# Polysketch attention with a gated causal convolution: contiguous loads, block transposes, 8-wide denominators, convolution on TensorE, and one written order of all steps

## The chip, the cores and the metric

The kernel runs on one core of a Trainium2 chip. The metric is the device time of one launch in microseconds (us). A core has five engines with their own instruction streams: TensorE (PE in the profile, with weight loads as PEld), VectorE (DVE), ScalarE (ACT), GpSimd (POOL) and SyncE (SP), which here issues the transfers. The profile counts sixteen DMA engines, which move the data. A transfer is started by an issue, an instruction on the queue of one engine; the data move afterwards. "SPq" and the like in a chain of waits is the time in which an engine's sequencer issues or holds instructions, as opposed to the data moving ("DMA"). PSUM holds the tiles into which the kernels have TensorE write; the changed kernel calls them banks. The profile also gives the clock that TensorE's throttle granted, 1.00 being full speed. The texts call 1.00 an open gate and 0.50 half clock.

Runs are labelled fast or slow, slow here being over 1.5% above the fastest of the same kernel.

## The reference, cut to what matters

```python
# q, k, v: (batch 4, heads 4, tokens 1088, dim 32); S1, S2: (8, 32)
def phi(x):                                   # 8 x 8 = 64 features a token and head
    a = einsum('rd,bhsd->bhsr', S1, x)
    b = einsum('rd,bhsd->bhsr', S2, x)
    return einsum('bhsi,bhsj->bhsij', a, b).reshape(..., 64)

q_p, k_p = phi(q), phi(k)
kv  = einsum('bhsf,bhsd->bhfd', k_p, v)       # 64 x 32 a head
z   = sum(k_p, axis=2)                        # 64 a head
num = einsum('bhsf,bhfd->bhsd', q_p, kv)
den = einsum('bhsf,bhf->bhs', q_p, z)[..., None] + 1e-06
x   = (num / den) -> (batch, tokens, 4 heads * 32 = 128)

gate = sigmoid(causal depthwise convolution of x, 5 taps per channel)
out  = (gate * (x @ w_val)) @ w_out           # float32, (4, 1088, 128)
```

The denominator has more structure than it shows: sum over i and j of a_i b_j z_ij is sum over i of a_i c_i with c = z b. So 64 products and a sum a token and head become 8, if c comes from a small product. The change uses this.

## The kernel before

Each batch is cut into nine chunks of up to 128 tokens. A chunk is loaded with tokens on partitions, in runs of 32 floats (128 bytes), transposed on TensorE and projected on TensorE. VectorE forms the 64 features per head, and TensorE sums k features times v over the chunks:

```python
for i in range(n_chunks):                      # 9 chunks a batch
    ...
    nc.sync.dma_start(out=q_shd[:sl, :, :], in_=src_q)      # 128-byte runs; k, v alike
    ...
    nc.tensor.transpose(k_dhs_p, k_shd..., identity32)      # float32 on TensorE
    nc.scalar.copy(out=k_dhs, in_=k_dhs_p)
    nc.tensor.matmul(ab_k_p[:sl, :], lhsT=k_dhs[:, :sl], rhs=S_blk)
    ...
    nc.vector.tensor_mul(k_p[:sl], a_bc[:sl], b_bc[:sl])
    for g in range(2):
        nc.tensor.matmul(kv_psums[g], lhsT=k_p..., rhs=v_ahd..., start=(i == 0), ...)
```

Only then, with z spread to all partitions, come the denominators, one reduction of 64 elements for each chunk and head, and the scaled features:

```python
for i in range(n_chunks):
    for h in range(H):
        nc.vector.tensor_tensor_reduce(out=tmp[:sl], in0=q_p_chunk[:sl, h, :],
                                       in1=z_bc[:sl, h, :], ..., accum_out=den[:sl, h : h + 1])
    nc.vector.reciprocal(rden[:sl], den[:sl])
    for h in range(H):
        nc.vector.tensor_scalar_mul(qps[:sl, h], q_p_chunk[:sl, h, :], rden[:sl, h : h + 1])
    for g in range(2):
        nc.tensor.transpose(qpt_p, qps..., identity)
        nc.scalar.copy(out=qpt_store[:, g, s0 : s0 + P], in_=qpt_p)
```

The convolution, the gate and the output of all four batches come at the end, the convolution as five passes over 1088 tokens on VectorE.

Of the kernel before, what the change touches and what calls it, by code (L numbers as in the profile page):

```python
# [13 lines left out]
ACT = mybir.ActivationFunctionType  # L15


@with_exitstack
def kernel(
# [12 lines left out]
    nc = tc.nc  # L32

# [4 lines left out]
    R2 = r * r  # L38
    HD = H * D
    Dm = moe_w_val.shape[0]  # L40
    assert Dm == HD == 128
    Kconv = moe_conv_w.shape[0]

    P = 128
    n_chunks = (S + P - 1) // P
    Sp = n_chunks * P
    chunk_sizes = [min(P, S - i * P) for i in range(n_chunks)]

    const = ctx.enter_context(tc.tile_pool(name="const", bufs=1))
    tmp_pool = ctx.enter_context(tc.tile_pool(name="tmp", bufs=2))  # L50
    sb = ctx.enter_context(tc.tile_pool(name="sb", bufs=5))
    psum = ctx.enter_context(tc.tile_pool(name="psum", bufs=5, space=bass.MemoryType.PSUM))
    kv_psum_pool = ctx.enter_context(tc.tile_pool(name="kv_psum", bufs=1, space=bass.MemoryType.PSUM))
    out_psum_pool = ctx.enter_context(
        tc.tile_pool(name="out_psum", bufs=1, space=bass.MemoryType.PSUM)
    )
    xpool = ctx.enter_context(tc.tile_pool(name="xpool", bufs=3))
    xsb_pool = ctx.enter_context(tc.tile_pool(name="xsb", bufs=B))

    def ptile(shape, dt=F32, tag="p0"):  # L60
        return psum.tile(shape, dt, tag="p0", name="p0")

    identity = const.tile([P, P], BF16)
    make_identity(nc, identity)
    identity32 = const.tile([P, P], F32)
    make_identity(nc, identity32)

    s1_sb = tmp_pool.tile([P, D], F32)
    nc.any.memset(s1_sb, 0.0)
    nc.sync.dma_start(out=s1_sb[:r, :], in_=S1)  # L70
    s1T_p = ptile([D, r], F32)
    nc.tensor.transpose(s1T_p, s1_sb[:r, :D], identity32[:r, :r])

    s2_sb = tmp_pool.tile([P, D], F32)
    nc.any.memset(s2_sb, 0.0)
    nc.sync.dma_start(out=s2_sb[:r, :], in_=S2)
    s2T_p = ptile([D, r], F32)
    nc.tensor.transpose(s2T_p, s2_sb[:r, :D], identity32[:r, :r])

    s12T = const.tile([D, 2 * r], F32)  # L80
    nc.vector.tensor_copy(out=s12T[:, :r], in_=s1T_p)
    nc.vector.tensor_copy(out=s12T[:, r:], in_=s2T_p)

    S_blk = const.tile([P, H * 2 * r], F32)
    nc.any.memset(S_blk, 0.0)
    for h in range(H):
        nc.sync.dma_start(
            out=S_blk[h * D : (h + 1) * D, h * 2 * r : (h + 1) * 2 * r],
            in_=s12T[:, :],
        )  # L90

    ones_row = const.tile([1, P], F32)
    nc.any.memset(ones_row, 1.0)

    w_val_sb = const.tile([Dm, Dm], BF16)
    nc.gpsimd.dma_start(out=w_val_sb, in_=moe_w_val)
    w_out_sb = const.tile([Dm, Dm], BF16)
    nc.gpsimd.dma_start(out=w_out_sb, in_=moe_w_out)

    conv_w_in = tmp_pool.tile([P, Dm], F32)  # L100
    nc.any.memset(conv_w_in, 0.0)
    nc.sync.dma_start(out=conv_w_in[:Kconv, :], in_=moe_conv_w)
    conv_wT_p = ptile([Dm, Kconv], F32)
    nc.tensor.transpose(
        conv_wT_p, conv_w_in[:Kconv, :Dm], identity32[:Kconv, :Kconv]
    )
    conv_wT = const.tile([Dm, Kconv], F32)
    nc.vector.tensor_copy(out=conv_wT, in_=conv_wT_p)

    eps = 1e-6  # L110

    x_sbs = []

    for b in range(B):
        kv_psums = [
            kv_psum_pool.tile([P, 2 * (D + 1)], F32, tag=f"kvp{g}", name=f"kvp{g}")
            for g in range(2)
        ]
        q_p_store = sb.tile([P, n_chunks, H, R2], F32, tag="qp_store")
        qpt_store = xpool.tile([P, 2, Sp], BF16, tag="qpt_store")  # L120

        for i in range(n_chunks):
            s0 = i * P
            sl = chunk_sizes[i]

            q_shd = sb.tile([P, H, D], F32, tag="q_shd")
            k_shd = sb.tile([P, H, D], F32, tag="k_shd")
            v_ahd = sb.tile([P, H, D + 1], F32, tag="v_ahd")
            if sl < P:
                nc.any.memset(q_shd, 0.0)  # L130
                nc.any.memset(k_shd, 0.0)
            nc.any.memset(v_ahd, 0.0)  # L132
            nc.gpsimd.memset(v_ahd[:sl, :, D : D + 1], 1.0)  # L133

            src_q = q[b, :, s0 : s0 + sl, :].transpose([1, 0, 2])
            src_k = k[b, :, s0 : s0 + sl, :].transpose([1, 0, 2])
            src_v = v[b, :, s0 : s0 + sl, :].transpose([1, 0, 2])
            nc.sync.dma_start(out=q_shd[:sl, :, :], in_=src_q)
            nc.sync.dma_start(out=k_shd[:sl, :, :], in_=src_k)
            nc.sync.dma_start(out=v_ahd[:sl, :, :D], in_=src_v)  # L140

            q_dhs_p = ptile([P, P], F32, tag="tp")
            nc.tensor.transpose(q_dhs_p, q_shd.rearrange("s h d -> s (h d)"), identity32)  # L143
            q_dhs = sb.tile([P, P], F32, tag="q_dhs")
            nc.scalar.copy(out=q_dhs, in_=q_dhs_p)  # L145

            k_dhs_p = ptile([P, P], F32, tag="tp")
            nc.tensor.transpose(k_dhs_p, k_shd.rearrange("s h d -> s (h d)"), identity32)  # L148
            k_dhs = sb.tile([P, P], F32, tag="k_dhs")
            nc.scalar.copy(out=k_dhs, in_=k_dhs_p)  # L150

            ab_q_p = ptile([P, H * 2 * r], tag="ab")
            nc.tensor.matmul(ab_q_p[:sl, :], lhsT=q_dhs[:, :sl], rhs=S_blk)  # L153
            ab_k_p = ptile([P, H * 2 * r], tag="ab")
            nc.tensor.matmul(ab_k_p[:sl, :], lhsT=k_dhs[:, :sl], rhs=S_blk)  # L155

            ab_q_ap = ab_q_p.rearrange("s (h rr) -> s h rr", h=H)
            b_q = sb.tile([P, H, r], F32, tag="b_q")
            nc.scalar.copy(out=b_q[:sl], in_=ab_q_ap[:sl, :, r:])  # L159
            q_p = q_p_store[:, i, :, :].rearrange("s h (i j) -> s h i j", i=r)  # L160
            a_bc = ab_q_ap[:, :, :r].unsqueeze(3).to_broadcast([P, H, r, r])
            b_bc = b_q[:, :, :].unsqueeze(2).to_broadcast([P, H, r, r])
            nc.vector.tensor_mul(q_p[:sl], a_bc[:sl], b_bc[:sl])  # L163

            ab_k_ap = ab_k_p.rearrange("s (h rr) -> s h rr", h=H)
            b_k = sb.tile([P, H, r], F32, tag="b_k")
            nc.scalar.copy(out=b_k[:sl], in_=ab_k_ap[:sl, :, r:])  # L167
            k_p = sb.tile([P, H, r, r], F32, tag="k_p")
            a_bc = ab_k_ap[:, :, :r].unsqueeze(3).to_broadcast([P, H, r, r])
            b_bc = b_k[:, :, :].unsqueeze(2).to_broadcast([P, H, r, r])  # L170
            nc.vector.tensor_mul(k_p[:sl], a_bc[:sl], b_bc[:sl])  # L171

            for g in range(2):
                nc.tensor.matmul(  # L174
                    kv_psums[g],
                    lhsT=k_p[:sl, 2 * g : 2 * g + 2, :, :].rearrange(
                        "s h i j -> s (h i j)"
                    ),
                    rhs=v_ahd[:sl, 2 * g : 2 * g + 2, :].rearrange("s h d -> s (h d)"),
                    start=(i == 0),  # L180
                    stop=(i == n_chunks - 1),
                    skip_group_check=True,
                )

        kv_bbs = [sb.tile([P, D], BF16, tag=f"kvbb{g}", name=f"kvbb{g}") for g in range(2)]
        z_col = sb.tile([P, 2], F32, tag="z_col")
        for g in range(2):
            nc.scalar.copy(out=kv_bbs[g][:R2, :], in_=kv_psums[g][:R2, :D])
            nc.scalar.copy(out=kv_bbs[g][R2:, :], in_=kv_psums[g][R2:, D + 1 : 2 * D + 1])
            nc.vector.tensor_copy(out=z_col[:R2, g : g + 1], in_=kv_psums[g][:R2, D : D + 1])  # L190
            nc.vector.tensor_copy(out=z_col[R2:, g : g + 1], in_=kv_psums[g][R2:, 2 * D + 1 : 2 * D + 2])

        z_p = ptile([2, P], F32, tag="tp")
        nc.tensor.transpose(z_p, z_col, identity32)
        z_p_sb = sb.tile([2, P], F32, tag="z_p_sb")
        nc.vector.tensor_copy(out=z_p_sb, in_=z_p)
        z4_row = sb.tile([1, H * R2], F32, tag="z4_row")
        nc.vector.tensor_copy(out=z4_row[:, : 2 * R2], in_=z_p_sb[0:1, :])
        nc.sync.dma_start(out=z4_row[:, 2 * R2 :], in_=z_p_sb[1:2, :])
# [6 lines left out]
        for i in range(n_chunks):  # L206
# [19 lines left out]
            if sl < P:  # L226
                nc.any.memset(qps[sl:, :, :], 0.0)
# [116 lines left out]
```

## Time and profile before

| | before |
|---|---|
| time, median of 3 runs | 197.38 us (197.37 to 197.38) |
| profiled span | 195.6 us |
| busy: TensorE / VectorE / ScalarE / GpSimd | 124.2 / 116.2 / 70.1 / 15.0 us |
| DMA packets | 59,545, nearly all under 512 B, 47 GB/s |

The runs agree within 0.01%. No engine is busy for much over 60% of the span, so the time lies in how the engines wait for one another. The lines that show it are in the prediction below.

### The profile page before, as it was taken

Reading aid. Unit: us, or ns where it says so; the run is one execution under the profiler, and the core shown is the slowest. Engines: PE = TensorE matmul, PEld = TensorE weight load, DVE = VectorE, ACT = ScalarE, POOL = GpSimd, SP = SyncE. Lnnn points to the kernel's source line nnn. Section 1 sums busy time; section 2 is a strip of 40 time slices with the busy share of each in tenths; the row PEclk is TensorE's granted clock in tenths of the full one; section 3 lists DMA queues with packets and bytes.
Section 4 is the critical chain, followed back from the end, with each engine's and each line's share of the span. In section 5 each row is a group of like instructions: output and inputs, shape, how many; then the busy total and the mean of one; then the engine's idle time right before and its main releaser. Section 6 shows DMA issues by size and latency. Waiting matters only on the chain.

```text
span 195.6 us, 2676 instructions
## 1 busy us (share of the span) xinstructions
PE 124.2 (63%) x542; PEld 90.0 (46%) x543; DVE 116.2 (59%) x626; ACT 70.1 (36%) x277; POOL 15.0 (8%) x89
## 2 busy tenths in 40 slices
PE   0129997255999962368899823669998245573650
PEld 0028995121689941124799610227997111232220
DVE  2014353399435575995434778965346969879650
ACT  3004342044534343345344222454342134342421
POOL 5002111000021110000111100000200000000000
DMA  4734353400142661001334620004210000013442
GB/s 61 119 58 64 50 80 52 71 11 0 28 68 42 98 96 19 0 0 23 61 48 78 108 32 0 0 2 70 44 29 3 0 0 0 2 54 89 113 121 82
DMA packets 59545, 9.16 MB, mean 47 GB/s; under 512 B 55173, under 2 KB 59530, under 8 KB 59530
## 3 DMA queue, kind: packets, MB, share of 16 engines
q1 hardware_dynamic: 59242, 8.94, 26.2%
q0 software_dynamic: 288, 0.07, 0.4%
q14 instruction: 11, 0.09, 0.2%
q8 instruction: 4, 0.07, 0.1%
HBM read 6.82 MB, written 2.23 MB: 46 GB/s over the span
## 4 chain that ended last, share of the span: by engine, by line
PE 43%; DVE 28%; DMA 12%; SPq 5%; ACT 5%; issue 4%; POOL 0%; ACTq 0%; POOLq 0%; DVEq 0%
PE kvp L174 14%; DVE qps L229 11%; DVE tmp L214 9%; PE p L153 8%; PE p L155 7%; DMA out_dram<-o_sb 4%; DMA z_row<-z_p_sb 3%; PE p L143 3%; DVE gate L286 3%; PE attn_p L250 3%; DMA k_shd<-in_k_dram 3%; PE p L148 3%; PE p L202 2%; SPq L313 2%; DVE rden L223 1%
## 5 line engine op out<-in xcount | busy, mean ns | idle before, releaser
L163 DVE TENSOR_TENSOR q_p_store<-p,b_q 128x256 f32<-128x256 f32 (+1 forms) x36 | 15.2, 423 | 42.1 <-ACT b_q L159 41.8
L174 PE MATMUL kvp<-v_ahd,k_p 128*128 128x66 f32 (+1 forms) x144 | 36.1, 407 | 2.3 <-POOL v_ahd L133 1.5
L234 PE MATMUL p<-identity,qps 128*128 128x128 bf16 x72 | 19.3, 290 | 27.2 <-DVE qps L229 26.2
L174 PEld LDWEIGHTS kvp<-v_ahd,k_p 128*128 128x128 f32 (+1 forms) x144 | 34.8, 331 | 3.4 <-POOL v_ahd L133 1.9
L214 DVE CUSTOM_DVE_ANT_0 tmp<-q_p_store,z_bc 128x64 f32<-128x64 f32 (+1 forms) x144 | 24.6, 213 | 9.3 <-ACT z_bc L204 9.3
L153 PE MATMUL p<-S_blk,q_dhs 128*128 128x64 f32 (+1 forms) x72 | 22.8, 419 | 9.4 <-DMA S_blk<-s12T 7.7
L239 ACT COPY qpt_store<-p 128x128 bf16<-128x128 bf16 x72 | 18.4, 268 | 26.7 <-PE p L234 25.1
L229 DVE TENSOR_SCALAR qps<-q_p_store,rden 128x64 bf16<-128x64 f32 (+1 forms) x144 | 26.7, 251 | 0.4
L234 PEld LDWEIGHTS <-qps 128*128 128x128 bf16 x72 | 6.9, 105 | 43.4 <-DVE qps L229 41.7
L153 PEld LDWEIGHTS p<-S_blk,q_dhs 128*128 128x128 f32 (+1 forms) x72 | 18.1, 312 | 14.0 <-issue 8.7
L155 PE MATMUL p<-S_blk,k_dhs 128*128 128x64 f32 (+1 forms) x72 | 22.2, 411 | 0.0
L286 DVE SCALAR_TENSOR_TENSOR gate<-x_sb,conv_wT,gate 128x1087 bf16<-128x1087 bf16 (+3 forms) x16 | 21.4, 1338 | 0.1
L155 PEld LDWEIGHTS p<-S_blk,k_dhs 128*128 128x128 f32 (+1 forms) x72 | 18.7, 320 | 0.4
L171 DVE TENSOR_TENSOR k_p<-p,b_k 128x256 f32<-128x256 f32 (+1 forms) x36 | 15.2, 423 | 5.7 <-ACT b_k L167 5.7
L159 ACT COPY b_q<-p 128x32 f32<-128x32 f32 (+1 forms) x36 | 6.6, 184 | 32.1 <-PE p L153 31.9
L143 PE MATMUL p<-identity,q_shd 128*128 128x128 f32 x36 | 15.2, 423 | 0.0
L148 PE MATMUL p<-identity,k_shd 128*128 128x128 f32 x36 | 15.2, 421 | 0.0
L132 POOL MEMSET v_ahd<- 128x132 f32 x31 | 6.5, 208 | 90.2 <-PE kvp L174 90.2
L145 ACT COPY q_dhs<-p 128x128 f32<-128x128 f32 x36 | 9.6, 268 | 6.5 <-PE p L143 3.8
L202 PE MATMUL p<-z_row,ones_row 1*128 1x256 f32 x8 | 4.7, 694 | 11.1 <-DMA z_row<-z_p_sb 11.1
L167 ACT COPY b_k<-p 128x32 f32<-128x32 f32 (+1 forms) x36 | 6.6, 184 | 14.2 <-PE p L155 14.1
L143 PEld LDWEIGHTS p<-identity,q_shd 128*128 128x128 f32 x36 | 11.6, 323 | 0.0
(57 smaller groups left out, 119.4 us busy)
## 6 DMA issues: line engine op xcount, KB each, us to landing
q_shd<-in_q_dram SPq DMA_DIRECT2D x32, 64.0 KB, 2.3
k_shd<-in_k_dram SPq DMA_DIRECT2D x32, 64.0 KB, 2.4
v_ahd<-in_v_dram SPq DMA_DIRECT2D x32, 64.0 KB, 2.2
out_dram<-o_sb SPq DMA_DIRECT2D x32, 64.0 KB, 1.6
q_shd<-in_q_dram SPq DMA_DIRECT2D x4, 32.0 KB, 2.2
k_shd<-in_k_dram SPq DMA_DIRECT2D x4, 32.0 KB, 2.3
v_ahd<-in_v_dram SPq DMA_DIRECT2D x4, 32.0 KB, 2.2
out_dram<-o_sb SPq DMA_DIRECT2D x4, 32.0 KB, 1.8
```

The lines of the kernel that those rows point to most:

```text
L143: nc.tensor.transpose(q_dhs_p, q_shd.rearrange("s h d -> s (h d)"), identity32)
L148: nc.tensor.transpose(k_dhs_p, k_shd.rearrange("s h d -> s (h d)"), identity32)
L153: nc.tensor.matmul(ab_q_p[:sl, :], lhsT=q_dhs[:, :sl], rhs=S_blk)
L155: nc.tensor.matmul(ab_k_p[:sl, :], lhsT=k_dhs[:, :sl], rhs=S_blk)
L163: nc.vector.tensor_mul(q_p[:sl], a_bc[:sl], b_bc[:sl])
L171: nc.vector.tensor_mul(k_p[:sl], a_bc[:sl], b_bc[:sl])
L174: nc.tensor.matmul(kv_psums[g], lhsT=k_p[:sl, 2 * g : 2 * g + 2, :, :].rearrange("s h i j -> s (h i j)"), rhs=v_ahd[:sl, 2 * g : 2 * g + 2 ...
L214: nc.vector.tensor_tensor_reduce(out=tmp[:sl], in0=q_p_chunk[:sl, h, :], in1=z_bc[:sl, h, :], scale=1.0, scalar=eps, op0=ALU.mult, op1=ALU ...
L229: nc.vector.tensor_scalar_mul(qps[:sl, h], q_p_chunk[:sl, h, :], rden[:sl, h : h + 1])
L234: nc.tensor.transpose(qpt_p, qps[:, 2 * g : 2 * g + 2, :].rearrange("s h f -> s (h f)"), identity,)
L239: nc.scalar.copy(out=qpt_store[:, g, s0 : s0 + P], in_=qpt_p)
L286: nc.vector.scalar_tensor_tensor(out=dst, in0=src, scalar=scal, in1=dst, op0=ALU.mult, op1=ALU.add,)
```

## The change

Its intent is to cut the fixed costs (many short instructions, of which those on VectorE took 215 or 252 ns for 64 elements and 425 for 256, and short DMA runs) and to let phases of different batches overlap. The diff rewrites the body; its core, with cuts marked by "...":

**Layout and loads.** A token's index is s = 34 m + t. A partition holds one head and one m (4 x 32 = 128) and, contiguous in memory, its 34 tokens of 32 floats. q and k come in two pieces each, of up to 3 KB a row; v is loaded head by head, with 512 B runs. Every batch has its own input buffers.

```diff
-            src_q = q[b, :, s0 : s0 + sl, :].transpose([1, 0, 2])
-            nc.sync.dma_start(out=q_shd[:sl, :, :], in_=src_q)
...
+        src = lambda x, t0, n: x[b].rearrange("h (m t) d -> (h m) (t d)", m=M)[:, t0 * D : (t0 + n) * D]
...
+            sync.dma_start(out=q_in[b][:, t0 * D : (t0 + n) * D], in_=src(q, t0, n))
...
+            for h in range(H):
+                sync.dma_start(
+                    out=v_in[b][:, u, h, :],
+                    in_=v[b, h].rearrange("(m t) d -> m (t d)", m=M)[:, u * 512 : u * 512 + 512]
+                    .rearrange("m (j x) -> j m x", j=4),
+                )
```

**Transposes** of 32 x 32 blocks on VectorE put head and dim on the partitions, many tokens in one instruction. **Features** of k are made on GpSimd, one 256-wide product for four tokens of every m.

```diff
-            nc.tensor.transpose(q_dhs_p, q_shd.rearrange("s h d -> s (h d)"), identity32)
-            nc.scalar.copy(out=q_dhs, in_=q_dhs_p)
+        nc.vector.transpose(
+            qT[b % 2][:, t0 : t0 + n, :].rearrange("p t m -> p (t m)"),
+            q_in[b][:, t0 * D : (t0 + n) * D],
+        )
```

**Denominators** are 8 wide: TensorE gives a, b and c = z b in one product per 128 tokens.

```diff
-                nc.vector.tensor_tensor_reduce(out=tmp[:sl], in0=q_p_chunk[:sl, h, :], in1=z_bc[:sl, h, :], ...)
...
+        nc.vector.tensor_mul(pden[i][:, :, 0:8], a_, csb[i].rearrange("p c (h i) -> p (c h) i", i=r))
+        nc.vector.tensor_reduce(out=den[i], in_=pden[i], axis=AX.X, op=ALU.add)
+        nc.vector.reciprocal(den[i], den[i])
+        nc.vector.tensor_mul(an[i], a_, bc(den[i], 2, [P, 12, 8]))
```

**Convolution** is five products with diagonal matrices, in two halves of 64 output channels. The other products are cut in halves, too, and the k-v product in quarters.

```diff
-                nc.vector.scalar_tensor_tensor(out=dst, in0=src, scalar=scal, in1=dst, op0=ALU.mult, op1=ALU.add)
...
+        for c in range(2):
+            nc.tensor.matmul(
+                o[64 * c : 64 * c + 64], lhsT=lhsT[:, 64 * c : 64 * c + 64], rhs=rhs, ...)
...
+        for t in range(Kconv):
+            mm64(o[:, 0 : n * M], diag[:, t, :], xe[b % 2][:, t0 + t : t0 + t + n, :]..., ...)
```

**Order.** A list of 355 steps gives the program order on all engines. A name is a kind, a batch and a piece (kp10 projects k of batch 1, gt01 convolves group 1 of batch 0; after the colon a PSUM bank). Steps of two or three batches are mixed. cn06 is ten dummy products of 512 columns at the very start.

```diff
+ORDER = """
+cn08 cn00 ld00 cn06 cn07 ld03 ld04 ld05 cn02 cn01 ld06 kt00 ld07 kp00
...
+kt20 nm01:2 kv19 qo02 xe01 kp20 ld36 pv10 pz10 qt12 gt01:0 ke20 kt21 ko20
...
```

**Stores** take 12 tokens of every m (10 in one group of three) from 128 partitions, whose order is j, then m:

```diff
+        nc.sync.dma_start(
+            out=dst[:, t0 : t0 + 4 * w, :].rearrange("m (j c) e -> j m (c e)", j=4),
+            in_=t[:, 0:w, :].rearrange("p c e -> p (c e)"),
+        )
```

## The prediction

> **What bounds the kernel now.** I read the page first, then a table of stretches, then the order of instructions where a stretch was dense, then the groups by form. Of the page:
>
> ```profile
> span 195.6 us, 2676 instructions
> ...
> PE 124.2 (63%) x542; PEld 90.0 (46%) x543; DVE 116.2 (59%) x626; ACT 70.1 (36%) x277; POOL 15.0 (8%) x89
> ...
> PE 43%; DVE 28%; DMA 12%; SPq 5%; ACT 5%; issue 4%; POOL 0%; ACTq 0%; POOLq 0%; DVEq 0%
> ```
>
> No engine is near 100%, and the chain that ended last passes through TensorE and VectorE by turns. The table of stretches shows why (columns: PE, weight loads, DVE, ACT, POOL busy us; clock; DMA share; GB/s):
>
> ```profile
> 0.00:13.00 13.00, 1.10 (x5) 0.66 (x5) 1.66 (x14) 2.23 (x6) 2.50 (x15) 1.00 0.52 77
> 13.00:33.00 20.00, 19.07 (x88) 17.75 (x88) 7.85 (x20) 7.86 (x38) 3.21 (x20) 1.00 0.44 68
> 33.00:53.00 20.00, 10.42 (x41) 4.61 (x41) 14.09 (x124) 7.06 (x28) 0.32 (x2) 1.00 0.17 26
> 53.00:72.00 19.00, 17.78 (x82) 16.56 (x82) 9.45 (x20) 7.09 (x35) 3.00 (x19) 1.00 0.47 74
> 72.00:92.00 20.00, 9.28 (x37) 3.91 (x38) 15.72 (x126) 9.09 (x28) 0.52 (x3) 1.00 0.06 9
> 174.00:196.00 22.00, 9.04 (x38) 3.72 (x37) 12.90 (x28) 5.48 (x18) 0.00 (x0) 1.00 0.37 102
> ```
>
> Each batch is two phases of about 20 us: loading, projecting and summing k (TensorE busy 19.07 of 20.00), then denominators, scaling and transposes of q (VectorE 14.09 to 15.72). They hardly overlap. Four batches of 40 us, 13 us before the first projection and some 20 us of convolution and output make the span. The start and the inside of a phase:
>
> ```profile
> 9.44 2.52 SPq L87 DMA_DIRECT2D S_blk<-s12T  x4
> ...
> 13.22 0.66 PE L153 MATMUL p<-S_blk,q_dhs 128*128 128x64 f32 x2 [7.65 <-DMA S_blk<-s12T]
> ...
> 14.11 0.42 PE L143 MATMUL p<-identity,q_shd 128*128 128x128 f32 x1
> ...
> 14.32 0.42 PE L148 MATMUL p<-identity,k_shd 128*128 128x128 f32 x1
> ...
> 15.79 1.07 PE L174 MATMUL kvp<-v_ahd,k_p 128*128 128x66 f32 x4
> ```
>
> TensorE waits 7.65 us for four small copies of the sketch. The four L174 records start (1.07 - 0.42)/3 = 0.22 us apart. A float32 product is two such records (144 for 72 calls), a transpose one.
>
> ```profile
> L229 DVE TENSOR_SCALAR qps<-q_p_store,rden 128x64 bf16<-128x64 f32 x128 | 23.7, 252 | 0.0
> L214 DVE CUSTOM_DVE_ANT_0 tmp<-q_p_store,z_bc 128x64 f32<-128x64 f32 x128 | 22.1, 215 | 9.3 <-ACT z_bc L204 9.3
> L234 PE MATMUL p<-identity,qps 128*128 128x128 bf16 x72 | 19.3, 290 | 27.2 <-DVE qps L229 26.2
> L163 DVE TENSOR_TENSOR q_p_store<-p,b_q 128x256 f32<-128x256 f32 x32 | 13.6, 425 | 40.9 <-ACT b_q L159 40.6
> L250 PE MATMUL attn_p<-qpt_store,kvbb 64*32 64x512 bf16 x32 | 7.5, 594 | 0.2
> L257 ACT CAST x_sb<-attn_p 128x512 bf16<-128x512 f32 x8 | 4.7, 585 | 5.6 <-PE attn_p L250 5.6
> ```
>
> VectorE does 144 reductions and 144 scalings of 64 elements each: mostly fixed cost.
>
> [...] So before seems to run at half clock, though the stretches say 1.00; the page has no clock row at all, so I trust the durations. [...] The change starts with ten dummy matmuls of 512 columns[...]. [...]at 24 us the rate is what it was at 13 us. [...] No row here shows two column tiles on the same rows. [...]GpSimd only clears buffers.
>
> **The change part by part.**
>
> VectorE, 116 us before. Gone: 144 reductions with their accumulator reads (24.6 + 11.7), 144 scalings (26.7), the convolution (21.4 + 2.0), 16 output copies, all of k's products beyond the first batch. New per batch[...]: block transposes of k 2 x 0.6 + 0.13, of q 1.34; denominators 3 x (0.26 multiply + 0.27 sum of 9 + 0.17 reciprocal + 0.26 multiply) = 2.9; products of q 3 x 0.95 (768 elements) = 2.85; gating 3 x 0.55 + 0.1 = 1.75. Sum 10.3, four batches 41, with 4 k products and constants 44 us.
>
> ScalarE, from its rows (0.268 for 128 elements, 0.585 for 512, so about 0.16 + 0.00083 N): per batch k copies 0.8, kv and z 0.7, z product 0.7, transposed features 3 x 0.77, x 1.4, sigmoid 1.45, output 1.6: 9. Total 36, with constants 39 us.
>
> GpSimd: 32 products of 0.62, constants 4: about 26 us, off the path.
>
> DMA: packets grow from 128 B to 512 to 2304 B, about 9,000 in place of 59,242. Every batch has its own input buffers, so all loads run ahead; 61 load issues at about 0.5 us (0.43 to 0.51 between issues early on) are 31 us of SyncE. Batch 0's last q piece is issue 19: 0.75 + 18 x 0.5 + 2.3 us landing = 12 us. So q work starts at about 12 us, when k of batch 0 is finished too. Off the path afterwards.
>
> TensorE, per batch, at the half clock seen. [...] Two records a product. If column tiles overlap in pairs (fours for kv): k 18 x 0.16 = 2.9; kv 72 records, 18 x 0.13 in fours, allow 3.2; z 0.5; preparing 0.6; q 18 x 0.21 = 3.85; 36 transposes 1.6; numerator 12, 1.6; convolution 15 pairs x 0.19 = 2.9 (5 taps, halved columns); value 0.6; output 0.8. Sum 18.5, four batches 74. The written order changes between tile modes 49 times[...]. Half clock: 84 us. Open gate: 40 + 8 = 48 us.
>
> The sum. Taking 12 us to the first q group with some 6 (9) us of TensorE work inside it, then the rest at 85% (92%) of the busiest engine, since one strict order must also cover cross-engine latencies, then 6.5 us for the drained tail and the last store (2 us), plus 1.8 us between span and time (197.38 - 195.6): open gate 12 + 42/0.85 + 8.3 = 70; half clock 12 + 75/0.92 + 8.3 = 102.
>
> **The rivals.** First, the clock. For an open gate: the dummy burst, and TensorE never idle for long. Against: dense float32 did not open it before, and much of the new work is float32 with short streams. Weight 55 to 30: 70 against 102 us. Second, column tiles don't overlap. For: every tile reads the same 128 rows, and in before only row tiles start together. Against: the change cuts every matmul in two halves, which would double its time. Open gate then gives some 95, half clock some 155; weight 10 and 5. Third, the order binds, not an engine: three rotating PSUM banks carry 52 uses, one bank the transposes, and each group passes twelve steps across engines. At 1.3 us a use this is 23 us on three banks, so it costs bubbles, not a bound; if it failed, open-gate TensorE would drop to 65% and 85 us result. Fourth, GpSimd's products slow down[...]: 9 per batch at even 1 us are still hidden.
>
> **Range and chances.** Between 70 and 102, the open gate likelier, with bubbles: I predict 79 us, and 66 to 105 for 8 times in 10. Slower needs both TensorE doubts to fall badly and bubbles on top.
>
> **What would show it.** Right: VectorE about 44 us, ScalarE 39, GpSimd 26 or more; TensorE the busiest or equal to VectorE; 128-column bf16 matmuls starting 0.055 apart, N = 384 latency near 0.33 (open) rather than 0.50 (half); first q product at about 12 us; packets near 9,000; chain mostly TensorE. Wrong: halves of one convolution tap starting a full stream apart; VectorE or ScalarE leading the chain; a DMA wait after 15 us; a k product on GpSimd above 1 us with TensorE waiting for it.

## The result, and the profile after

| | before | after |
|---|---|---|
| median | 197.38 us | 83.37 us |
| all runs of after | | 84.87 (slow), 83.08, 83.66 (slow), 82.39 us |
| ratio of fast runs, 95% interval | | 0.419 (0.417 to 0.421) |
| clock of these runs | | 0.815, 0.861, 0.873, 0.876 |

Ratios, here and below, are the mean time of one kernel's fast runs over that of the other's of the same rounds, so not quite the ratio of the medians that stand beside them. The profile of after below is of the run of 84.87 us; it is 3% above the fastest, so it serves for where the time lies and not for differences of a few per cent. The outputs of both kernels agree with the reference.

The page of the changed kernel, the lines that answer to those shown of before; the rows of digits are 40 slices of the span, in tenths busy (PEclk: tenths of full clock):

```profile
span 83.1 us, 2652 instructions
...
PE 60.0 (72%) x1083; PEld 42.7 (51%) x1083; DVE 43.8 (53%) x115; ACT 35.3 (42%) x92; POOL 23.7 (29%) x56
...
PE   3977548497944999975990699999989999760000
...
PEclk9999975555795558999999555999999999998555
DMA  0362347822449336932384222000212202222220
...
SPq 36%; PE 28%; DMA 16%; ACT 3%; issue 3%; DVE 2%; ACTq 0%; DVEq 0%
```

VectorE's 626 instructions of before became 115, TensorE's 542 became 1083 with half the busy time. From the 24th slice on TensorE is at 9 nearly throughout, which is what the written order is for. But the chain that ended last names TensorE for 28% only: 52% is SyncE's issuing and transfers. In the last slices the DMA row stands at 2 while every engine rests. The same in the table of stretches (columns as in the prediction):

```profile
0.00:12.00 12.00, 7.91 (x102) 4.14 (x102) 5.46 (x14) 2.29 (x4) 6.14 (x23) 0.98 0.34 102
12.00:30.00 18.00, 13.46 (x252) 10.55 (x252) 10.42 (x27) 6.29 (x19) 6.06 (x12) 0.59 0.55 172
30.00:46.00 16.00, 12.28 (x261) 9.01 (x257) 10.70 (x28) 7.89 (x19) 7.84 (x14) 0.93 0.55 168
46.00:62.00 16.00, 15.14 (x302) 11.39 (x304) 9.13 (x26) 8.90 (x27) 3.42 (x7) 0.80 0.16 48
62.00:76.00 14.00, 11.20 (x180) 7.59 (x176) 8.07 (x22) 9.96 (x24) 0.29 (x1) 1.00 0.23 70
76.00:83.10 7.10, 0.00 (x0) 0.00 (x0) 0.00 (x0) 0.00 (x0) 0.00 (x0) 0.52 0.20 70
```

Three things are to be seen. TensorE is at 15.14 of 16.00 us only after the loads are over (46 us); up to then it has bubbles, with the DMA engines at 0.55 of their time, though they reach 1.00 from 25 to 26 us. In the last row nothing but DMA runs for 7.1 us, at a share of 0.20. And the clock in the second row, 0.59, is between half and open. The chain in order of time (start us, us, what) shows what the first 46 us hang on:

```profile
27.12 1.17 SPq L220
...
30.03 4.95 DMA v_in<-in_v_dram
34.99 0.62 SPq L220
```

L220 issues a v load. So the chain goes through issues of v, one after another, and then through a v transfer of 4.95 us. From 46.9 us on the chain is nearly all TensorE pieces. SyncE's own order (start, duration, what), first a row of v issues, then the last stores:

```profile
13.95 6.37 SPq L220 DMA_DIRECT2D v_in<-in_v_dram  x8
...
72.85 2.85 SPq L470 DMA_DIRECT2D out_dram<-osb  x3
75.80 0.54 SPq L475 DMA_DIRECT2D out_dram<-osb  x1
```

Eight issues take 6.37 us, or 0.80 each, where the prediction read 0.43 to 0.51 in before; the four rows of eight together take 24.7 us (5.58 + 6.37 + 5.93 + 6.84), and SyncE issues loads with hardly a pause until 42.8 us. The last store is issued at 75.80 and the span ends at 83.1. ScalarE's last copy ended at 75.04 + 0.26 = 75.30.

Two readings lie open. **A:** v loads and stores are written with an outermost dimension of 4 (the "j" in front), and they may keep no more than about four DMA engines busy. In the stretches of the trace where only stores move, the DMA share is 0.20 to 0.28, and where only v loads move it is 0.29 at 86 to 87 GB/s (18 to 21, 30 to 31.9 and 37 to 40 us): four of sixteen engines are 0.25. From 25 to 26 us, soon after q and k loads were issued (21.56 to 24.75 us), it is 1.00 at 372 GB/s. **B:** SyncE issues too much, 77 transfers of mostly 0.43 us or more each, and the data wait for their issue. In the chain alone B looks stronger (36% against 16%). The first four experiments set the two against each other.

### The profile page after: what moved, and what is told of

The parts are those of the page before. It is cut to its first block, busy times and chain, and to the rows that moved or that the text cites. A ratio compares the mean times of both kernels' runs of the same rounds, so it can differ in the third digit from the quotient of the medians.

```text
span 83.1 us, 2652 instructions
## 1 busy us (share of the span) xinstructions
PE 60.0 (72%) x1083; PEld 42.7 (51%) x1083; DVE 43.8 (53%) x115; ACT 35.3 (42%) x92; POOL 23.7 (29%) x56
## 2 busy tenths in 40 slices
DMA packets 10126, 9.25 MB, mean 111 GB/s; under 512 B 1917, under 2 KB 8578, under 8 KB 10114
## 3 DMA queue, kind: packets, MB, share of 16 engines
q1 hardware_dynamic: 10114, 9.08, 35.4%
## 4 chain that ended last, share of the span: by engine, by line
SPq 36%; PE 28%; DMA 16%; ACT 3%; issue 3%; DVE 2%; ACTq 0%; DVEq 0%
SPq L220 23%; PE ring L137 12%; DMA v_in<-in_v_dram 11%; SPq L233 5%; DMA v_lo<-in_v_dram 5%; PE pt L364 4%; PE qab L333 3%; SPq L216 3%; SPq L227 3%; PE kv L285 3%; ACT gate L410 2%; PE ring L381 2%; PE ring L443 2%; PE kab L258 1%; DVE phi L353 1%
## 5 line engine op out<-in xcount | busy, mean ns | idle before, releaser
L275 POOL TENSOR_TENSOR phik<-kab_sb 128x256 f32<-128x256 f32 x32 | 19.8, 651 | 24.0 <-ACT kab_sb L268 22.5
L137 PE MATMUL ring<-xe,diag 128*64 128x384 bf16 (+1 forms) x120 | 12.8, 347 | 0.7 <-ACT xe L390 0.4
L285 PE MATMUL kv<-phik,v_in 128*32 128x64 f32 x256 | 10.3, 258 | 2.2 <-DMA v_in<-in_v_dram 2.1
L373 ACT COPY phiT<-pt 128x768 bf16<-128x768 bf16 (+1 forms) x12 | 9.2, 766 | 6.1 <-PE pt L364 5.9
L353 DVE TENSOR_TENSOR phi<-an,qab 128x768 bf16<-128x768 f32 x12 | 11.2, 934 | 0.0
L364 PE MATMUL pt<-ident,phi 128*64 128x128 bf16 (+1 forms) x144 | 7.4, 240 | 3.7 <-DVE phi L353 3.6
L333 PE MATMUL qab<-wq,qT 128*64 128x96 f32 x144 | 9.0, 271 | 0.3 <-ACT wq L316 0.3
L258 PE MATMUL kab<-wq,kT 128*64 128x64 f32 x144 | 7.8, 271 | 1.6 <-ACT kab_sb L268 1.0
L137 PEld LDWEIGHTS <-diag 128*64 128x64 bf16 x120 | 7.1, 119 | 3.5 <-issue 1.3
L333 PEld LDWEIGHTS qab<-wq,qT 128*64 128x64 f32 x144 | 7.3, 151 | 1.0 <-ACT wq L316 0.6
```

The source lines that it names most:

```text
L137: nc.tensor.matmul(o[64 * c : 64 * c + 64], lhsT=lhsT[:, 64 * c : 64 * c + 64], rhs=rhs, start=start, stop=stop, skip_group_check=True,)
L258: nc.tensor.matmul(o[64 * z : 64 * z + 64, :, c, :], lhsT=kT[b % 2][:, two[z] : two[z] + 2, :].rearrange("p t m -> p (t m)"), rhs=wq[0][:, ...
L275: eng.tensor_mul(phik[u][:, c].rearrange("p h (i j) -> p h i j", i=r), bc(a_, 3, [P, H, r, r]), bc(b_, 2, [P, H, r, r]),)
L285: nc.tensor.matmul(bank_kv[32 * h : 32 * h + 32, 0:64], lhsT=lt, rhs=phik[u][:n, c, h, :], start=i == 0, stop=i == 9, skip_group_check=Tru ...
L333: nc.tensor.matmul(o[64 * z : 64 * z + 64, :, c, :], lhsT=qT[b % 2][:, two[z] : two[z] + 2, :].rearrange("p t m -> p (t m)"), rhs=wq[b % 2 ...
L353: nc.vector.tensor_mul(phi[i].rearrange("p c (i j) -> p c i j", i=r), bc(an[i], 3, [P, 12, r, r]), bc(b_, 2, [P, 12, r, r]),)
```

## The experiments

All kernels gave the right output. "The change" is the changed kernel. Four runs each, unless said otherwise (five for the stores with m outermost); runs on one chip share their runs of before (medians 197.35 to 197.40 us). Three chips were used, so kernels are compared by their ratios to before.

### 1 to 4: transfers on four engines, or issues of SyncE?

**v split by j and not by head.** The same number of issues, bytes and 512 B runs, but 32 rows outermost:

```diff
-            for h in range(H):
-                sync.dma_start(out=v_in[b][:, u, h, :],
-                    in_=....rearrange("m (j x) -> j m x", j=4))
+            for j in range(4):
+                sync.dma_start(out=v_in[b][32 * j : 32 * j + 32, u, :, :],
+                    in_=v[b].rearrange("h (m t) d -> m h (t d)", m=M)[:, :, u * 512 + j * 128 : u * 512 + j * 128 + 128])
```

> The 32 loads of v are cut by block of rows (32 partitions, outermost dimension 32) in place of by head (128 partitions, outermost dimension 4). Same number of issues, same bytes, same 512-byte runs. Theory A (a transfer whose outermost dimension is 4 runs on 4 of the 16 DMA engines, and these four hold back the first 46 us): waits of TensorE and VectorE for v and q shrink to under 5 us in all, time 72 to 77 us against 83. Theory B (the number of issues on SyncE, 61 at 0.5 us, sets the pace): unchanged within 1.5 us, 82 to 85. Theory C (TensorE and its clock set the pace): unchanged, 82 to 84.

**Stores with m outermost.** The gating product writes its result in the order (m, j), so that a store begins with 32 m's and not with 4 j's; v as in the change:

```diff
-            gv[i][:, 0:f].rearrange("p (c j m) -> p j c m", c=w, j=4),
+            gv[i][:, 0:f].rearrange("p (c m j) -> p j c m", c=w, j=4),
...
-            out=dst[...].rearrange("m (j c) e -> j m (c e)", j=4),
+            out=dst[...].rearrange("m (j c) e -> m j (c e)", j=4),
```

> Rows inside a block are ordered so that the outermost dimension of a store is 32 in place of 4; loads as in the change. Theory A: the 7.1 us in which only stores ran at the end fall to about 3, stores no longer share four engines with v, time 77 to 80. Theory B and C: the same issues and the same TensorE work, so at most the last store shortens, 82 to 84.

**Both.**

> Both of the above. Theory A: the gains add, 66 to 72 us, and TensorE becomes the busiest over the whole span with the DMA waits gone. Theory B: 82 to 84. Theory C: 81 to 84.

**v issued by ScalarE**, still with four outermost, which takes 32 of SyncE's 77 issues away:

```diff
-                sync.dma_start(
+                nc.scalar.dma_start(
                     out=v_in[b][:, u, h, :],
```

> The loads of v are as in the change (outermost dimension 4) but issued from ScalarE's queue, so SyncE has 45 issues in place of 77. Theory A: no gain, as the same four engines carry the same bytes: 81 to 86, with ScalarE held up in issuing. Theory B: 73 to 78.

| | median (range), us | ratio to before | against the change |
|---|---|---|---|
| the change | 83.37 (82.39 to 84.87) | 0.419 | |
| v split by j | 76.52 (74.99 to 79.30) | 0.382 (0.380 to 0.384) | 8.9% less |
| stores m outermost | 81.55 (80.50 to 82.77) | 0.409 (0.408 to 0.410) | 2.5% less |
| both | 73.44 (71.87 to 74.44) | 0.366 (0.364 to 0.369) | 12.6% less |
| v issued by ScalarE | 90.62 (90.14 to 91.56) | 0.458 (0.456 to 0.460) | 9.4% more |

The last column divides the ratios: 0.3817 / 0.4191 = 0.911, and so on; the medians of all runs give 8.2, 2.2 and 11.9% less and 8.7% more. Only v split by j fell into its range under A. The others missed theirs on the slow side (stores 77 to 80, both 66 to 72, v on ScalarE 81 to 86).

The packets, too, speak for A's premise that more engines take part. The DMA line of the change, then with v split by j:

```profile
DMA packets 10126, 9.25 MB, mean 111 GB/s; under 512 B 1917, under 2 KB 8578, under 8 KB 10114
```

```profile
DMA packets 10510, 9.25 MB, mean 126 GB/s; under 512 B 2301, under 2 KB 8962, under 8 KB 10498
```

For the same bytes there are 384 more packets, all under 512 B: 12 for each of the 32 loads. With the stores m outermost there are 200 more (10,326): 12 for each of the 12 large stores and 14 for each of the four small ones, which had 2 outermost. Twelve is 16 less 4, and 14 is 16 less 2: the counts would fit one more packet for each engine that takes part. This is the author's reading; no view says which engine a packet ran on.

B falls only in part. The number of issues is not what counts: with the same number the time fell by 8.9%, and with 32 fewer on SyncE it rose by 9.4%. But their length changed with the pattern. All issues of v in the change, then with v split by j (ns: shortest/median/longest):

```profile
L220 SPq DMA_DIRECT2D v_in<-in_v_dram x32: 528/632/1918, 3.3 to 39.1; - x32
```

```profile
L220 SPq DMA_DIRECT2D v_in<-in_v_dram x32: 312/430/1271, 3.3 to 31.3; - x32
```

The row of eight that took 6.37 us now reads:

```profile
12.46 3.75 SPq L220 DMA_DIRECT2D v_in<-in_v_dram  x8
```

All four rows went from 24.7 to 18.0 us, and the last load was issued by 35.4 us and not by 42.8. Part of the "SPq 36%" thus belongs to the pattern itself: even the shortest issue is longer, and from ScalarE's queue (below) the pattern with 4 takes a median of 537 ns. The rest is held time, of up to 1.9 us in one issue. For the loads the runs do not part fewer engines from longer issues; the pattern with 4 outermost brings both, the share of 0.29 and the median of 632 ns. For the stores they do: the issues are equally long in both forms (medians 537 and 539 ns), and only the time after the last one fell, as shown below.

Who waits for q, in the change and in the kernel with v split by j (engine, line, released by: us in total, times, longest):

```profile
DVE qT L321 <- DMA q_in<-in_q_dram: 11.7, 6, 4.6
```

```profile
DVE qT L322 <- DMA q_in<-in_q_dram: 3.3, 2, 2.9
```

VectorE's waits for q fell by 8.4 us although the q loads were not touched: they stood behind the v loads and their issues. With v issued from ScalarE, still with 4 outermost, VectorE's waits for q are gone from the list, and the loading stretch moves more than in the change (there 0.55 and 172 GB/s):

```profile
12.00:30.00 18.00, 7.56 (x137) 5.98 (x136) 5.52 (x14) 3.25 (x12) 3.00 (x6) 0.50 0.77 245
```

So SyncE's queue did hold the loads back, as B says. The kernel is slower all the same, and what the trace shows for it is ScalarE's own work held up behind v (its longest wait there; two more such lines have 6.6 and 6.0 us):

```profile
ACT kab_sb L268 <- DMA v_in<-in_v_dram: 10.1, 2, 7.9
```

The fourth experiment thus moves the issues in front of the work of an engine that others wait for, and is no test of B alone.

With both changes the stretches look so (columns as before):

```profile
12.00:30.00 18.00, 14.10 (x274) 10.86 (x276) 12.55 (x31) 6.84 (x19) 8.20 (x15) 0.74 0.75 221
30.00:46.00 16.00, 15.29 (x380) 11.50 (x378) 12.98 (x34) 9.53 (x26) 8.60 (x15) 1.00 0.45 130
...
68.60:69.60 1.00, 0.00 (x0) 0.00 (x0) 0.00 (x0) 0.00 (x0) 0.00 (x0) 0.84 0.53 164
```

The DMA share in the loading stretch went from 0.55 to 0.75 and the rate from 172 to 221 GB/s; in 1 us with a store alone it is 0.53 at 164 GB/s, where the change has 0.20 at 70 over its last 7.1 us and 0.26 at 94 from 77 to 79 us. TensorE is full from 30 us on and not from 46. The last issue ends at 68.66 us and the span at 71.0: 2.3 us, where the change has 83.1 - 76.34 = 6.8.

The stores alone shorten the tail as much (their last issue ends at 78.46 us and the span at 80.8, in a run of the same clock, 0.817, as the profiled one of the change), but that issue comes 2.1 us later than in the change, and VectorE is busy for 47.7 us and not 43.8. The gating product pays for the new order. The group of that product in the change, and then in the kernel with both (columns: busy us, mean ns | idle before it):

```profile
L426 DVE TENSOR_TENSOR gv<-gate,ring 128x384 bf16<-128x384 bf16 x8 | 4.4, 547 | 4.8 <-PE ring L137 1.9 <-ACT kvb L317 1.5 <-ACT gate L410 1.3
```

```profile
L427 DVE TENSOR_TENSOR gv<-gate,ring 128x384 bf16<-128x384 bf16 x8 | 8.1, 1011 | 4.3 <-ACT gate L411 2.7 <-ACT kvb L318 1.6
```

Its 2-byte results now lie 8 bytes apart, and it takes 1011 ns in place of 547. Two further kernels try to get round that.

### 5 and 6: other ways to widen the stores

**Inputs strided, output in order.** Both changes, but the product walks the output in its order in memory and picks the inputs with a stride:

```diff
-            gv[i]....rearrange("p (c m j) -> p j c m", ...), gate[i]....rearrange("p (j c m) -> p j c m", ...), ...
+            gv[i]....rearrange("p (c m j) -> p c m j", ...), gate[i]....rearrange("p (j c m) -> p c m j", ...), ...
```

> As e3_both, but the gating product walks its output in order and its two inputs with strides, where e3_both wrote 2-byte elements 8 bytes apart and the gating rose from 0.55 to about 0.95 us. If the strided write is what cost: gating back at 0.55, VectorE at 43.5 us busy, time 1 to 3 us under e3_both, so 70 to 72. If any stride costs: 73 to 75, as e3_both.

**Four stores of 32 rows each** in place of one of 4 x 32, on top of v split by j; 56 store issues, those of the last batch shared between SyncE and ScalarE:

```diff
+        for j in range(4):
+            eng = nc.scalar if b == 3 and j % 2 else nc.sync
+            eng.dma_start(out=dst[:, t0 + j * w : t0 + j * w + w, :]..., in_=t[32 * j : 32 * j + 32, 0:w, :]...)
```

> e1_v16 with each store cut into four by block of 32 rows ([...]56 issues in place of 16), the last batch's shared between SyncE and ScalarE; the gating product as in the change. If e3_both's slower gating took back part of its gain: VectorE at 43.5, the tail as in e3_both, 69 to 72 us. If the added issues of about 0.45 us hold the stores back: 73 to 77.

The first gave 72.57 us (70.73 to 73.98); only one run was fast, so there is no ratio, and its range overlaps that of the kernel with both (71.87 to 74.44): not told apart, and the expectations (70 to 72, or 73 to 75) do not decide either. The product itself did get cheaper, to 803 ns and not to the 0.55 us hoped for:

```profile
L427 DVE TENSOR_TENSOR gv<-gate,ring 128x384 bf16<-128x384 bf16 x8 | 6.4, 803 | 4.0 <-ACT gate L411 2.9 <-PE ring L137 1.1
```

The second gave 73.99 us (73.51 to 75.23), ratio 0.374 (0.373 to 0.375): 2.0% under v split by j alone, against 4.1% for m outermost (0.3662 / 0.3817). This is the weaker remedy, in the range expected if the 40 added issues cost time (73 to 77).

### 7: what the written order is worth

The change's own steps, all loads issued first, then each batch's steps one after another, with nothing of another batch between them:

```diff
-kt20 nm01:2 kv19 qo02 xe01 kp20 ld36 pv10 pz10 qt12 gt01:0 ke20 kt21 ko20 ...
+... kt20 kt21 kp20 ke20 kp21 ke21 ko20 kv20 ko21 kv21 kz20 ... qt20 qp20 qc20 qd20 qo20 qx20 qe20 nm20 xe20 ...
```

> The change with every step, shape and buffer kept, but the steps written in plain order: all loads first as in the change, then each batch from k to the output, one step after the other, the rotating PSUM banks in turn. If the interleaved order is a large part of the gain: each engine waits for the next, busy times stay (VectorE 44, ScalarE 35, GpSimd 24), time 110 to 150 us. If loads on four DMA engines set the pace whatever the order: 85 to 95.

It took 165.67 us (165.55 to 165.74), ratio 0.839 (0.838 to 0.841), far above the 110 to 150 expected. The groups of a batch, too, follow one another here, so the order within a batch is part of what was taken away. A stretch of it with 268 of its 1083 TensorE instructions, so about one batch:

```profile
57.00:93.00 36.00, 21.66 (x268) 13.75 (x268) 10.44 (x26) 8.72 (x21) 5.59 (x10) 0.50 0.06 17
```

And one of its waits, 12 times in the run, once for each of the three groups of a batch:

```profile
DVE pden L320 <- ACT csb L315: 35.3, 12, 3.3
```

VectorE's work fell from 116 to 46 us, and the batch from 40 to 36 us: the steps themselves are worth 197.4 - 165.7 = 31.7 us, their order 165.7 - 83.4 = 82.3 us. Each step waits for the one before on another engine, and in the plain order nothing else is there to do. The order does two things that this run does not part: it fills those waits, and TensorE runs at a higher clock in it. In the plain order the granted clock was 0.52 in the profiled run and the same 1083 TensorE instructions took 91.0 us; in the written order 0.815 and 60.0. TensorE's longer times can account for 31.0 us at most (91.0 - 60.0), so some 51 of the 82.3 us or more are filled waits (estimate from these numbers).

### 8 and 9: the clock

**No dummy products**, on v split by j:

```diff
-cn08 cn00 ld00 cn06 cn07 ...
+cn08 cn00 ld00 cn07 ...
```

> e1_v16 without the ten dummy matmuls. If the burst is what opens the gate: the clock row stands at 5 until the convolutions start at about 25 us, and the k products before it take twice as long; since TensorE waits for loads there, 1 to 4 us slower than e1_v16 (76.5). If the gate opens by the real work alone, or if loads hide all of it: within 1 us of e1_v16.

**A burst in the kernel before**: 16 dummy products of 512 columns in bfloat16 ahead of each batch.

```diff
+        for t in range(16):
+            dummy = ptile([P, 512], F32)
+            nc.tensor.matmul(dummy, lhsT=zero[:, :P], rhs=zero)
```

> The kernel before with 16 dummy matmuls of 512 zero columns put ahead of each batch (16 x 0.43 us at half clock, 0.21 with an open gate). If the kernel before ran at half clock throughout, the gate opens, a clock row appears, the 0.213 us spacing of its float32 records falls to about 0.107 while the gate holds, and the time falls to 160 to 190 us in spite of the added work. If float32 work closes the gate again within a few us, or 0.213 is the float32 rate at any clock: 198 to 215 us.

Without the burst: 75.36 us (74.76 to 75.83), ratio 0.382 (0.380 to 0.384), the same as with it to the last digit shown; up to 4 us slower, or no change, had been expected. Ten dummy products at the start took 4.45 us with the burst (from 1.26 us, in v split by j). TensorE's order after that, first with the burst, then without (start, us, what):

```profile
7.36 0.80 PE L259 MATMUL kab<-wq,kT 128*64 128x64 f32 x20 [0.47 <-ACT kab_sb L269]
```

```profile
7.46 1.34 PE L259 MATMUL kab<-wq,kT 128*64 128x64 f32 x20 [0.47 <-ACT kab_sb L269]
```

The burst makes TensorE faster here: the same 20 records take 0.80 us with it and 1.34 without. It buys nothing, presumably since the work waits for loads at this time anyway. There is a trap here. The clock row of the kernel without the burst reads 9 in these slices, although 1.34 us is the slow rate:

```profile
PEclk9999999999999999999999999999999999999855
```

So a 9 in that row, or a 1.00 in a table of stretches, can only be trusted together with the durations; in the kernel before they disagreed as well (1.00 listed, 0.22 us between records), and one run in plain order lists 1.00 where the other three have 0.52 to 0.53, at the same 165.6 to 165.7 us.

The burst in the kernel before gave 196.72, 202.53, 197.06 and 203.33 us, two of its runs slow; before had 197.40. This lies between the two ranges expected (160 to 190, 198 to 215). The clock was 0.59 to 0.62. In the profiled run the gate was open for a while after a burst. Four records of the k-v product in that stretch take 0.56 us where they took 1.07 in before:

```profile
20.73 0.56 PE L180 MATMUL kvp<-v_ahd,k_p 128*128 128x66 f32 x4
```

The four start (0.56 - 0.28) / 3 = 0.09 us apart, if the last took the 0.28 of the transpose records beside it, against 0.22 in before. So float32 records, too, ran faster for a while after a burst. The 13 dummy products of one burst in that run took 3.06 us, those of another 4.20. The fast runs gained 0.3% by it, but they also carry the dummy products, 20.8 us of TensorE's busy time; what the open gate alone would be worth there is not shown. Why two of these runs were 3% longer is open.

### 10: are the halves worth it?

v split by j, with each pair of 64-column halves as one 128-column product (convolution, value, output, one of z's):

```diff
-        for c in range(2):
-            nc.tensor.matmul(o[64 * c : 64 * c + 64], lhsT=lhsT[:, 64 * c : 64 * c + 64], rhs=rhs, ...)
+        nc.tensor.matmul(o, lhsT=lhsT, rhs=rhs, ...)
```

> e1_v16 with the convolution, value, output and z matmuls in one piece of 128 columns in place of two of 64. If halves overlap in pairs (the prediction's working case; the trace has ten halves of 384 columns in 1.02 us, 0.145 us a pair): no stream time is gained[...], so 0.5 to 4 us slower than e1_v16. If halves run one after the other (the second rival): convolution halves from about 1.0 to 0.5 us open gate, 4 to 8 us faster.

It took 77.06 us (75.88 to 77.47), ratio 0.387 (0.384 to 0.389), against 0.382: 1.3% slower, and not the 4 to 8 us faster that halves one after the other would have meant. Halves do overlap. A piece of the chain in the change, ten records of 384 columns, which are five taps in two halves:

```profile
70.92 1.02 PE ring L137 x10
```

The convolution's records have a median of 326 ns. Five pairs take 1.02 us, so pairs start (1.02 - 0.33) / 4 = 0.17 us apart. The two halves of a value product, of 384 columns too, take 0.35 us together (from 70.16 us), where one such record has a mean of 333 ns, so they run almost wholly side by side. A wide product gains nothing: its records of 384 columns have a mean of 352 ns, the halves in v split by j 328. What the 1.3% comes from, no run shows.

### 11: the convolution left on VectorE

v split by j, with the five taps as in the kernel before, on groups of up to 384 tokens:

```diff
-            mm64(o[:, 0 : n * M], diag[:, t, :], xe[...], start=t == 0, stop=t == Kconv - 1)
+            nc.vector.scalar_tensor_tensor(out=o, in0=x, scalar=cwT[:, t : t + 1], in1=o, op0=ALU.mult, op1=ALU.add)
```

> e1_v16 with the convolution on VectorE, as before did it: one scaling and four multiply-adds for each of 12 groups, some 0.46 us each. VectorE rises from 43.5 to about 68 us busy, TensorE falls by some 11. If VectorE's load then binds: 82 to 92 us. If TensorE is what binds e1_v16 after the loads: 70 to 76.

It took 103.29 us (101.36 to 104.88) against 76.52; only one run was fast, so there is no ratio, but the ranges are far apart. This is more than the 82 to 92 expected. Its costliest form on VectorE, and the stretch in the middle of the run:

```profile
L408 DVE SCALAR_TENSOR_TENSOR cv<-xe,cwT,cv 128x384 bf16<-128x384 bf16 x32 | 21.3, 665 | 1.1
```

```profile
46.00:90.00 44.00, 25.07 (x367) 17.61 (x367) 39.39 (x90) 17.87 (x46) 6.71 (x11) 0.58 0.11 31
```

A tap takes 665 ns and not the 0.46 us put in; with the 16 shorter ones four of the five taps are 30.4 us, and VectorE is busy for 76.3 us of a span of 101.7. From 46 to 90 us it is at 39.39 of 44.00 us, and it leads the chain (49%, TensorE 8%): VectorE binds there. The granted clock fell to 0.64, with TensorE at 25.07 of the same 44.00 us. How much the convolution on TensorE gains by the lower clock, beside the work taken off VectorE, the run does not part.

### 12: the best version

Both changes with strided inputs, no dummy products, and a small v load of batch 2 moved ahead of the loads of batch 3, where the order of the change had left it behind; six runs:

```diff
-... ld39 ko23 ld27 om01:0 ...
+... ld26 ld27 qd01 ... ld39 ko23 om01:0 ...
```

> e5_st16c without the dummy matmuls and with batch 2's last small load of v moved ahead of batch 3's loads. If what is left in the first half is TensorE waiting for single late loads: 69 to 71.5 us (e5_st16c: 72.6). If the loads as a whole, at some 220 GB/s between 12 and 30 us, set the pace whatever their order: 72 to 74, as e5_st16c.

71.82 us (70.94 to 74.35), ratio 0.3598 (0.3591 to 0.3605): 14.1% less than the change (0.3598 / 0.4191) and correct. Against the kernel with strided inputs alone the ranges overlap, so the moved load and the missing burst are not shown to gain; 71.82 lies between the two ranges expected (69 to 71.5, 72 to 74).

## Why the prediction was right or wrong

The total, 79 us with 66 to 105, holds 83.37. Step by step:

| step | predicted | measured |
|---|---|---|
| VectorE busy | 44 us | 43.8 |
| ScalarE busy | 39 us | 35.3 |
| GpSimd busy, one product | 26 us, 0.62 us | 23.7, 0.651 |
| TensorE busy | 48 open, 84 half | 60.0 (plain order at 0.52: 91.0; no burst, clock listed as 0.971: 52.0) |
| packets | about 9,000 | 10,126 |
| first q work | 12 us | 14.28 (first q product 16.52) |
| DMA after that | off the path | on it until 46 us |
| last store | 2 us | 6.8 from its issue's end (76.34 to 83.1) |

**Right: what bounded before.** The plain order shows it most clearly: with less than half of VectorE's work but phases still in series the time is 165.7 us. And TensorE did run below its full rate, though the stretches said 1.00: the 0.22 us between records became 0.09 after a burst.

**Right: the costs of VectorE and GpSimd.** The sums were met within 1% and 10%; ScalarE's was 10% too high. Most of VectorE's terms lie near a line through two of before's rows, 425 ns for 256 elements and 684 for 512, which gives 0.26 us for 96, 0.55 for 384 and 0.94 for 768 (estimate); measured are 0.24 to 0.26, 0.547 and 0.934. The block transposes, 0.6 for one of k (measured 0.701), and GpSimd's 0.62 were estimates, for which before has no row. The fourth rival (slower products on GpSimd) fell with 651 ns a product, the mean of its 32. Two of the prediction's sums are slightly off (18 x 0.21 is 3.78 and not 3.85; VectorE's terms add to 10.2 and not 10.3), which changes nothing.

**Right: halves overlap.** The second rival fell with 0.17 us a pair, and with wide products that gained nothing. The median of 326 ns of the convolution's records is the 0.33 us that the prediction named for an open gate; in the plain order, at a clock of 0.50, those of 384 columns have a mean of 527 ns where it named 0.50 us.

**Right, with a reserve: the order is no bound.** The third rival said that banks and twelve-step groups leave TensorE at 65%. It is at 72% of the span, but 15.14 of 16.00 us from 46 to 62 us. The bubbles of the first 46 us went largely with the loads: with both changes it is at 15.29 of 16.00 from 30 us on.

**Wrong: "Off the path afterwards."** The prediction counted 61 issues at about 0.5 us, 16 us for the 32 of v, and looked only at packets, not at how many DMA engines a transfer keeps busy. v loads with four outermost moved at a DMA share of 0.29, their issues took 24.7 us, and q stood behind them. The loads' issues ended at 42.8 us and not at 31. Two of the prediction's own signs show it: a DMA wait after 15 us came (the chain has a v transfer of 4.95 us from 30.03 on), and the chain is not mostly TensorE (28%, SyncE 36%). Splitting v by j took back 8.9%. The hint was in the diff: the "j" in front of the pattern.

**Wrong in size: the last store.** After its issue it took 6.8 us and not the 2 assumed, at a DMA share of 0.26 from 76 to 80 us; with m outermost it was 2.3.

**Wrong: a gate that is open or half.** It was both in one run, 0.59 in one stretch and 0.93 in the next. And the burst, taken for a sign of an open gate, gains nothing here: ratio 0.382 with and without.

So the 79 us came near partly by luck. It was a mean between a kernel at open and one at half clock; the kernel measured had stretches of both, and DMA waits on the path that neither sum held. By the prediction's own weights the mean would have been 86 us (0.55 x 70 + 0.30 x 102 + 0.10 x 95 + 0.05 x 155).

**Open:** how much of the order's 82 us is the clock (31 at most, by the estimate above); whether the v loads lost by fewer engines or by longer issues; what lowers the clock between 12 and 30 us (0.59); whether a change of tile mode costs anything (the prediction's 84 and 48 us for TensorE hold 10 and 8 us for 49 of them, estimate, not measured; its times for single products, 0.13 to 0.21 us at half clock, were estimates too); how far the 8.9% of the v loads came through a higher clock (0.895 in the profiled run, against 0.861 and 0.876 in fast runs of the change).

## What to carry to other kernels

Shorter and fewer instructions pay little while each waits for the one before on another engine: here the steps gave 32 us and their order 82 us. When loads are taken off the critical path on paper, read the access pattern of each transfer for its outermost dimension, not only its packet size; putting 32 there in place of 4 gave 12.6%. And do not take issue time for a constant: it depended on the pattern (median 0.63 against 0.43 us), and moving the issues to an engine with work of its own made the kernel 9.4% slower.
